# Cosine attention and a leaky-ReLU MLP on one core: another order of the norms, loads and score tiles around the first two batches

## The chip, the cores and the metric

The kernel runs on one core of a Trainium2 chip. The metric is the device time of one execution in microseconds (us). The engines are TensorE (PE), VectorE (DVE), ScalarE (ACT), GpSimd (POOL) and SyncE (SP); each takes its instructions in the order in which the kernel writes them. DMAs are issued by SP and GpSimd (and a few at the start and end by ACT) and run on the core's 16 DMA engines.

## The reference

```python
q, k, v: (8, 12, 448, 64)     # batch, heads, tokens, head_dim, float32
q_n = q / (norm(q, axis=-1) + 1e-6);  k_n = k / (norm(k, axis=-1) + 1e-6)
scores = matmul(q_n, k_n.T) / tau                       # tau = 0.1
attn = exp(scores - max) ; attn = attn / (sum + 1e-9)
a = matmul(attn, v)                                     # per head
x = a.transpose(0, 2, 1, 3).reshape(3584, 768)
h = x @ w_in                                            # 768 x 2048
out = maximum(0.01 * h, h) @ w_out                      # 2048 x 768, float32
```

## The kernel before

The unit of the attention is a *pair* of heads, numbered `s` from 0 to 47: six pairs to a batch (`NPAIR` = 6). Three *slots* `j` of two pairs each make up a batch (`NQ` = 3). A head's 448 tokens are three tiles of 128 keys and a remainder of 64; the remainders of two pairs share one tile. The order of all instructions is written out by hand, and the helpers only record them.

What is done for a pair:

- **Loads.** `load_qk(s)` issues four DMAs on SP (L142, L143, L145 twice) into one of six places of `raw_sb`. `load_pairs(eng, x, part, s, n)` loads the same for `n` pairs at once, on any engine (L127, L132).
- **Norm.** `squares(s)` on GpSimd (L182), `sums(s)` on DVE (L193), `roots(s)` on ACT in two steps (L200, L201), `normalise(s)` on DVE (L217, L218, L222 twice). For pairs from 10 on, `transposes(s)` is one DMA transpose issued by SP (L254) into `qkT[s]`. `norm(s)` records roots, normalise and transposes, then the loads of a later pair, then `hold` (a small GpSimd copy, L514, that makes GpSimd wait for the normalise), then the squares of the pair two further on.
- **Scores.** `key_tiles([(s, ki), ...])` records the score matmuls (L280) and, for each tile, an Exp on ACT (L292) to `pe`, or to `pr` for the remainder tile (`ki` = 3, of pairs `s − 1` and `s`). Each tile takes two PSUM banks from `banks(2)`, which gives out the banks that were used longest ago.
- **Products.** For a slot: `totals` (sums of the Exps by ones, L320), `reciprocals` (ACT Ln and Exp, L339 and L340), `products` with v (L320) and `scale` (DVE, L361) into `xT`. `attend_two(j)` does two slots at once, the remainder products first (`rem_products`, L307), which read `v_rem`.

The MLP works on eight chunks of tokens, alternately 384 and 512 wide, one for each batch. `firsts(b)` are the first products (L384) of chunk `b`, in 16 steps `m`, with a leaky ReLU on ACT (L391); with each step it can call other functions, by the dictionary `between`. `visit(b, ...)` are the second products (L459) of chunk `b` in groups of two 64-row halves, and between their steps the score tiles of the batch `b + 1`; `norms[i, n]` are functions called after step `n` of group `i`, and `wide`, `three`, `four`, `four_late` say after which steps a score tile stands. At a group's end its rows are copied to `osb` (DVE L471, for the last group one of two on ACT L471) and stored by SP (L436).

So the loop over the batches is: `visit(b)`, `attend_batch(b + 1)`, the loads of v (GpSimd, L160 and L167), `firsts(b + 1)`. Ahead of it stand the first batch's attention and `firsts(0)`. There, slot 2's first two MLP tiles are begun early: `begin(m, kts)` records a few of the six accumulating matmuls of tile `m`, for which the first slots' results suffice.

Before the change, pair 12 and 13 are loaded by SP in `norm(11)`, in the first visit; 14 and 15 in `attend_batch(1)`, where `norm(12)` stands too. Pairs 13 to 16 are normalised during `firsts(1)`, pair 17 in the second visit, whose last remainder tile `(17, 3)` comes at its end and whose schedule is `four_late`. From the third visit on, all remainder tiles stand at a visit's start.

Of the kernel before, what the change touches and what calls it, by code (L numbers as in the profile page):

```python
# [16 lines left out]
def kernel(  # L17
# [21 lines left out]
    NQ = NPAIR // 2  # L39
    KT = D_model // 128  # L40
# [4 lines left out]
    SOON = 4  # L45
# [20 lines left out]
    gp = nc.gpsimd  # L66
# [70 lines left out]
    def load_qk(s):  # L137
        if s >= NSLOT:
            return
        b, h0 = s // NPAIR, 2 * (s % NPAIR)  # L140
        both = raw_sb[:, s % NPAIR]
        nc.sync.dma_start(out=both[:, :, 0:3], in_=main(q, b, h0, 2))  # L142
        nc.sync.dma_start(out=both[:, :, 4:7], in_=main(k, b, h0, 2))  # L143
        for i, x in enumerate((q, k)):
            nc.sync.dma_start(  # L145
                out=both[64 * i : 64 * i + 64, :, 3],
                in_=x[b, h0 : h0 + 2, MAIN:S].rearrange("h p d -> p h d"),
            )
        raw[s] = (both[:, :, 0:4], both[:, :, 4:7])
# [36 lines left out]
    def sums(s, parts=(0, 1)):  # L186
        if s >= NSLOT:
            return
        if s not in ss:
            ss[s] = smp.tile([128, 14], F32, name="ss")  # L190
        for i in parts:
            o = ss[s][:, 0:8] if i == 0 else ss[s][:, 8:14]
            nc.vector.tensor_reduce(  # L193
                o.rearrange("p (h t) -> p h t", h=2), sqs[s][i], axis=AX.X, op=ALU.add
            )

    def roots(s):
        if s >= NSLOT:
            return
        nc.scalar.activation(ss[s], ss[s], func=AF.Ln, bias=tiny)  # L200
        nc.scalar.activation(ss[s], ss[s], func=AF.Exp, scale=0.5)  # L201
# [63 lines left out]
    def scores(s, kis):  # L265
        key_tiles([(s, ki) for ki in kis])

    def key_tiles(which):

        tiles = []  # L270
        for s, ki in which:
            sc = banks(2)
            tiles.append(sc)
            for i in range(2 if ki == 3 else 1):
                x = qkT[s - 1 + (i ^ s // 2 % NQ % 2)] if ki == 3 else qkT[s]
                for a in range(2):
                    rows = slice(64 * a, 64 * a + 64)
                    out = sc[64 * i : 64 * i + 64] if ki == 3 else sc
                    c0, c1 = (448, 512) if ki == 3 else (512 + 128 * ki, 640 + 128 * ki)
                    nc.tensor.matmul(  # L280
                        out=out[:, a, :S], lhsT=x[rows, c0:c1], rhs=x[rows, 0:S],
                        start=True, stop=True,
                    )
        for (s, ki), sc in zip(which, tiles):
            if ki == 3:
                pr[s // 2] = prp.tile([128, 2, S], BF16, name="pr")
                dst = pr[s // 2]
            else:
                if s not in pe:
                    pe[s] = pep.tile([128, 3, 2, S], BF16, name="pe")  # L290
                dst = pe[s][:, ki]
            nc.scalar.activation(out=dst, in_=sc[:, :, :S], func=AF.Exp, scale=inv_tau)  # L292
# [344 lines left out]
    def begin(m, kts):  # L637

        if (0, m) not in pms:
            pms[0, m] = banks(1, (0, m, 0))  # L640
        first(0, m, kts)

    scores(5, (0, 1))
    products(1, 1)
    for m in range(2):
        begin(m, range(2))
    for e in range(2):
        scale(1, e)
    scores(5, (2,))
    for m in range(2):  # L650
        begin(m, range(2, KT - 2))
    scores(5, (3,))
    for m in range(2, SOON):
        pms[0, m] = banks(1, (0, m, 0))
    begin(2, range(KT - 2))
    sums(6)
    sums(7)
    roots(6)

    def attend(j, behind=()):  # L660
        totals(j)
        reciprocals(j)
        po = banks(2)
        for e in range(2):
            products(j, e, po[:, e])
        for fn in behind:
            fn()
        for e in range(2):
            scale(j, e)
# [18 lines left out]

    def attend_batch(b):
        if b == 1:  # L690
            load_qk(14)
            load_qk(15)
            sums(12)
        attend_two(b * NQ)
        if b == 1:
            norm(12)
        attend(b * NQ + 2)


    def norm(s, transposed=True):  # L700
        if s >= NSLOT:
            return
        roots(s)
        normalise(s)
        if transposed:
            transposes(s)
        if s == 10:
            return
        for x in (12, 13) if s == 11 else (s + 4,) if s > 11 else ():
            load_qk(x)  # L710
        hold(qn[s][:, 6, 0, 0:1])
        if s == 11:
            squares(12)
        if s != 9:
            squares(s + (3 if s < 9 else 2))
# [11 lines left out]
    def visit(b, order, norms, between):  # L727


        s0 = (b + 1) * NPAIR  # L730
        tiles = [(s0 + p, ki) for p in range(NPAIR) for ki in range(3)]
        key_tiles([(s0 + 1, 3), (s0 + 3, 3)] + [(s0 + 5, 3)] * (b > 1))
        for i, (pairs, after) in enumerate(zip(order, between)):
            last = i == len(order) - 1
            for n, _ in enumerate(groups(b, pairs, 4 if len(pairs) > 1 else 1, last), 1):
                for _ in range(after.get(n, 0)):
                    key_tiles([tiles.pop(0)])
                for fn in norms.get((i, n), ()):
                    fn()
        assert not tiles  # L740
        if b < 2:
            key_tiles([(s0 + 5, 3)])

    def at(*steps):
        return {n: steps.count(n) for n in steps}
# [1 line left out]
    wide = (at(8, 13, 18, 24, 29, 35, 40, 45, 50, 55, 60), at(4, 8, 12, 16, 16, 21, 26))  # L747
    three = (at(9, 16, 16, 21, 26, 31), at(5, 10, 16, 16, 21, 26, 31), at(5, 10, 16, 16, 20))
    four = (at(9, 16, 16, 24), at(4, 10, 16, 16, 24), at(4, 10, 16, 16, 24), at(5, 10, 16, 16))
    four_late = (at(5, 11, 16, 16, 24),) * 3 + (at(6, 16, 16),)  # L750

    deals["apart"] = False
    attend(NQ - 1, [lambda m=m: first(0, m, range(KT - 2)) for m in range(3, SOON)])
    normalise(6)
    hold(xT[0][:, 2 * NQ - 2, 0:1])
    load_w_out(range(0, MT, MT // 4))
# [8 lines left out]
            8: [lambda: transposes(7)],  # L765
            9: [lambda: norm(9, False)],
            10: [lambda: transposes(8)],
            11: [lambda: sums(10), lambda: load_v(3)],
            12: [lambda: norm(10), lambda: load_v(4)],
            13: [lambda: transposes(9), lambda: load_v(5), lambda: load_v_rem(1)],  # L770
            15: [lambda: sums(11)],
        },
# [1 line left out]
    ready = 10  # L774
    for b in range(B):
        tokens = chunk_cols(b)[1] // 128
        if b == B - 1:
            for ts in range(tokens):
                for half in range(2):
                    second(b, ts, half)  # L780
            break
        order = [[((ts, 0), (ts, 1))] for ts in range(tokens)]
        if b == 0:
            order = [order[0] + order[1], order[2]]
        norms = {(0, 18): [lambda: norm(11)]}
        if b:
            norms = {}
            for i in range(tokens - 1 + (b == 1)):
                norms[i, 4 if tokens > 3 else 12] = [lambda s=ready: norm(s)]
                ready += 1  # L790
                norms[i, 20] = [lambda s=ready: sums(s)]
        else:
            ready += 2
        visit(
            b, order, norms,
            wide if b == 0 else four_late if b == 1 else three if tokens == 3 else four,
        )
        attend_batch(b + 1)
        for j in range((b + 2) * NQ, (b + 3) * NQ):
            load_v(j)  # L800
        load_v_rem(b + 2)
        s = ready
        between = {0: [lambda s=s: norm(s)], 1: [lambda s=s: sums(s + 1)]}
        if b == 0:
            between = {
                0: [lambda: sums(13)], 1: [lambda: norm(13), lambda: sums(14)],
                4: [lambda: norm(14), lambda: sums(15)], 7: [lambda: norm(15)],
                9: [lambda: sums(16)], 11: [lambda: norm(16)], 14: [lambda: sums(17)],
            }
            ready += 5  # L810
        elif tokens == 3:
            between.update({
                4: [lambda s=s: norm(s + 1), lambda s=s: sums(s + 2)],
                7: [lambda s=s: norm(s + 2), lambda s=s: sums(s + 3)],
                10: [lambda s=s: norm(s + 3)], 13: [lambda s=s: sums(s + 4)],
            })
            ready += 4
        else:
            between.update({
                4: [lambda s=s: norm(s + 1)], 5: [lambda s=s: sums(s + 2)],  # L820
                8: [lambda s=s: norm(s + 2)], 12: [lambda s=s: sums(s + 3)],
            })
            ready += 3
        firsts(b + 1, 0, between)
# [35 lines left out]
```

## Time and profile before

| | us |
|---|---|
| median of 3 runs (lowest to highest) | 407.20 (407.15 to 407.24) |
| profiled execution | 407.09 |
| its span | 405.3 |
| PE busy (share of the span) | 398.5 (98%) |
| ACT busy | 265.0 (65%) |
| DVE busy | 187.7 (46%) |
| GpSimd busy | 140.7 (35%) |

Where the stretches that the diff touches lie in the span: the last slot's scores of batch 0 and the early MLP products from 28 to 36 us; `firsts(0)` from 36 to 50; the first visit from 50 to 70; `attend_batch(1)` from 70 to 76.7; `firsts(1)` from 76.8 to 97.6; the second visit from 97.6 to 122.7.

How to read it: the profile is of one execution, and the time around the span (407.09 − 405.3 = 1.8 us) belongs to each run. Busy times are shares of the whole span; what an edit is worth is read in its own stretch, by what the instructions there wait for. A row of a timeline is start, duration, engine, line, operation, output and inputs with their shapes, the number of merged instructions, and in brackets idle time just before it and what ended that. `q0` is GpSimd's DMA queue, `q1` that of SP.

### The profile page before, as it was taken

How to read it: one execution, taken by the hardware profiler on the slowest of the kernel's cores; microseconds unless marked ns; L12 is line 12 of the kernel's file. 1: busy time of each engine (PE TensorE's matmuls, PEld its weight loads, DVE VectorE, ACT ScalarE, POOL GpSimd, SP SyncE). 2: the span in 40 equal slices, each digit the busy share in tenths (PEclk: the TensorE clock that was granted, in tenths of full speed). 3: DMA queues.
4: the chain of work that ended last, by engine and by line, in shares of the span. 5: the costliest groups of instructions: out<-in, count | busy, mean ns of one | idle time of the engine just before them, and what ended most of it. 6: DMA issues, size and time to landing. Idle time of an engine off the chain costs nothing.

```text
span 405.3 us, 10173 instructions
## 1 busy us (share of the span) xinstructions
PE 398.5 (98%) x4096; PEld 225.0 (56%) x4096; DVE 187.7 (46%) x403; ACT 265.0 (65%) x458; POOL 140.7 (35%) x215
## 2 busy tenths in 40 slices
PE   8999999999999999999999999999999999999996
PEld 3335655544555655544886555544687555544564
DVE  6987912684665624454452626256361731130021
ACT  5996799556874689654876569745786559844300
POOL 4995823363344513343141513255122500000000
PEclk9999999999999999999999999999999999999999
DMA  7999999697689826576486844686477721110033
GB/s 190 252 227 246 214 184 212 180 182 180 147 195 154 153 60 175 118 126 174 73 185 142 131 113 118 160 117 152 68 177 125 96 45 40 40 41 2 0 78 79
DMA packets 100735, 54.21 MB, mean 134 GB/s; under 512 B 69424, under 2 KB 95440, under 8 KB 100688
## 3 DMA queue, kind: packets, MB, share of 16 engines
q1 hardware_dynamic: 76400, 40.13, 42.0%
q0 software_dynamic: 23440, 12.92, 23.2%
q8 instruction: 32, 0.52, 0.5%
q10 hardware_dynamic: 848, 0.52, 0.4%
q14 instruction: 15, 0.12, 0.1%
HBM read 45.61 MB, written 11.01 MB: 140 GB/s over the span
## 4 chain that ended last, share of the span: by engine, by line
PE 93%; POOL 3%; DVE 1%; DMA 1%; issue 1%; ACT 0%; POOLq 0%
PE ps L384 36%; PE ps L459 31%; PE ps L320 11%; PE ps L280 8%; PE ps L421 5%; POOL sq L182 1%; PE ps L307 1%; DMA raw_sb<-in_k_dram 1%; POOL v_rem L167 1%; DVE qn L222 1%; PE ps L236 1%; POOL raw_sb L132 0%; POOL v_b L160 0%; POOL seen L514 0%; DVE qkT L261 0%
## 5 line engine op out<-in xcount | busy, mean ns | idle before, releaser
L384 PE MATMUL ps<-xT,w_in_sb 128*128 128x384 bf16 (+1 forms) x768 | 148.0, 353 | 0.0
L459 PE MATMUL ps<-w_out_sb,hT 64*128 64x384 bf16 x1536 | 144.0, 323 | 0.0
L292 ACT ACTIVATE pe<-ps 128x896 bf16<-128x896 f32 x144 | 124.5, 917 | 17.2 <-PE ps L280 15.3
L384 PEld LDWEIGHTS <-w_in_sb 128*128 128x128 bf16 x768 | 74.0, 98 | 71.7 <-issue 4.0
L391 ACT ACTIVATE hT<-ps 128x384 bf16<-128x384 f32 (+1 forms) x128 | 67.2, 544 | 66.6 <-PE ps L384 66.1
L459 PEld LDWEIGHTS <-hT 64*128 64x128 bf16 x1536 | 84.4, 94 | 44.8 <-PE ps L459 4.2
L182 POOL TENSOR_TENSOR sq<-raw_sb 128x512 f32<-128x512 f32 x90 | 82.4, 937 | 12.5 <-DMA raw_sb<-in_k_dram 11.9
L222 DVE TENSOR_TENSOR qn<-raw_sb,r 128x512 bf16<-128x512 f32 x96 | 56.6, 631 | 2.0 <-DMA raw_sb<-in_q_dram 0.3
L280 PE MATMUL ps<-qkT 64*128 64x448 bf16 (+1 forms) x384 | 54.8, 353 | 1.1 <-DVE qkT L261 0.6
L193 DVE TENSOR_REDUCE ss<-sq 128x6 f32<-128x384 f32 (+1 forms) x95 | 54.3, 610 | 1.1 <-POOL sq L182 1.0
L471 DVE COPY osb<-ps 128x384 f32<-128x384 f32 x41 | 21.2, 553 | 69.7 <-PE ps L459 38.8
L514 POOL CAST seen<-qn 128x1 f32<-128x1 bf16 x46 | 9.1, 198 | 124.3 <-DVE qn L222 124.0
L217 DVE TENSOR_SCALAR ss<-ss 128x14 f32<-128x14 f32 x48 | 10.2, 213 | 75.7 <-ACT ss L201 75.6
L361 DVE TENSOR_TENSOR xT<-ps,rb 128x448 bf16<-128x448 f32 x48 | 27.8, 620 | 24.6 <-ACT rb L340 24.4
L160 POOL DMA_DIRECT2D v_b<-in_v_dram x24 | 18.6, 776 | 39.6 <-PE ps L320 39.6
L320 PE MATMUL ps<-pe,v_b 128*32 128x448 bf16 x576 | 32.0, 353 | 0.0
L280 PEld LDWEIGHTS <-qkT 64*128 64x128 bf16 (+1 forms) x384 | 17.7, 97 | 17.6 <-issue 7.3
L339 ACT ACTIVATE rb<-ps 128x448 f32<-128x448 f32 x24 | 12.9, 538 | 14.9 <-PE ps L320 13.9
L320 PEld LDWEIGHTS <-v_b 128*32 128x32 bf16 x576 | 15.1, 97 | 12.0 <-issue 0.6
L427 DVE COPY osb<-ps 128x384 f32<-128x384 f32 (+1 forms) x9 | 4.6, 513 | 36.6 <-PE ps L421 36.6
L421 PE MATMUL ps<-w_out_sb,hT 128*128 128x384 bf16 (+1 forms) x144 | 21.0, 308 | 0.0
L292 ACT ACTIVATE pr<-ps 128x896 bf16<-128x896 f32 x24 | 20.7, 924 | 0.2 <-PE ps L280 0.2
(52 smaller groups left out, 188.2 us busy)
## 6 DMA issues: line engine op xcount, KB each, us to landing
raw_sb<-in_q_dram SPq DMA_DIRECT2D x46, 192.0 KB, 3.2
raw_sb<-in_k_dram SPq DMA_DIRECT2D x44, 192.0 KB, 3.2
out_dram<-osb SPq DMA_DIRECT2D x30, 192.0 KB, 3.0
v_b<-in_v_dram POOLq DMA_DIRECT2D x24, 192.0 KB, 4.9
out_dram<-osb SPq DMA_DIRECT2D x12, 384.0 KB, 2.6
w_out_sb<-in_moe_w_out_dram POOLq DMA_DIRECT2D x4, 768.0 KB, 15.8
w_in_sb<-in_moe_w_in_dram POOLq DMA_DIRECT2D x3, 512.0 KB, 8.4
w_in_sb<-in_moe_w_in_dram POOLq DMA_DIRECT2D x2, 768.0 KB, 12.7
```

The lines of the kernel that those rows point to most:

```text
L182: eng.tensor_tensor(sq, x, x, op=ALU.mult)
L193: nc.vector.tensor_reduce(o.rearrange("p (h t) -> p h t", h=2), sqs[s][i], axis=AX.X, op=ALU.add)
L222: scalings[s] = nc.vector.tensor_tensor(qn[s][:, lo:hi], x.rearrange("p h t d -> p t h d"), r[:, r0 : r0 + 2 * nt].rearrange("p (h t) -> p ...
L280: nc.tensor.matmul(out=out[:, a, :S], lhsT=x[rows, c0:c1], rhs=x[rows, 0:S], start=True, stop=True,)
L292: nc.scalar.activation(out=dst, in_=sc[:, :, :S], func=AF.Exp, scale=inv_tau)
L320: nc.tensor.matmul(out=x[32 * g : 32 * g + 32, :S], lhsT=weights(g, ki) if ki < 3 else rem(g), rhs=pe[s][:, ki, a, :] if ki < 3 else pr[j] ...
L361: scalings[j, e] = nc.vector.tensor_tensor(xT[m][:, 2 * jj + e, half * S : (half + 1) * S], pos.pop((j, e))[:, :S], rbs[j], op=ALU.mult,)
L384: nc.tensor.matmul(out=pm[:, :n], lhsT=w_in_sb[:, kt, m * 128 : (m + 1) * 128], rhs=xT[c // 2][:, kt, c0 : c0 + n], start=(kt == 0), stop= ...
L391: nc.scalar.activation(out=hT[c][:, m, :n], in_=pms.pop((c, m))[:, :n], func=AF.Prelu, alpha=0.01)
L421: nc.tensor.matmul(out=po2[:, :n], lhsT=hT[c][:, m, ts * 128 : (ts + 1) * 128], rhs=w_out_sb[:, m, lo : lo + n], start=(m == 0), stop=(m = ...
L459: done[p][i] = nc.tensor.matmul(out=pos2[p][:, i, :HALF], lhsT=hT[c][rows, m, ts * 128 : (ts + 1) * 128], rhs=w_out_sb[rows, m, half * HAL ...
L471: copy(out=osb[c, ts][:, half * HALF : (half + 1) * HALF], in_=po2[:, i, :HALF])
```

## The change

It has four parts. In the head, the scores of slot 2 come ahead of some of the early MLP products, and `roots(6)` is recorded after the slot's `attend`. Pairs 12 and 13 are loaded by GpSimd in `firsts(0)` at step 11, ahead of v and v_rem, with four DMAs of two pairs each; `norm(11)` then loads 14 and 15 on SP, so that `attend_batch(1)` loads nothing. The norms move up by one place: `sums(12)` and `norm(12)` into the second group of the first visit (steps 6 and 14), 13 into `attend_batch(1)`, 14 to 17 into `firsts(1)`. The second visit then takes all three remainder tiles first, normalises three pairs instead of four, and has the schedule `four` of the later visits.

```diff
     scores(5, (0, 1))
     products(1, 1)
-    for m in range(2):
-        begin(m, range(2))
+    begin(0, range(2))
     for e in range(2):
         scale(1, e)
     scores(5, (2,))
-    for m in range(2):
-        begin(m, range(2, KT - 2))
+    begin(1, range(2))
+    begin(0, range(2, KT - 2))
     scores(5, (3,))
+    begin(1, range(2, KT - 2))
     for m in range(2, SOON):
         pms[0, m] = banks(1, (0, m, 0))
-    begin(2, range(KT - 2))
+    begin(2, range(2))
     sums(6)
     sums(7)
-    roots(6)
...
         if b == 1:
-            load_qk(14)
-            load_qk(15)
-            sums(12)
+            sums(13)
         attend_two(b * NQ)
         if b == 1:
-            norm(12)
+            norm(13)
         attend(b * NQ + 2)
...
-        for x in (12, 13) if s == 11 else (s + 4,) if s > 11 else ():
+        for x in (14, 15) if s == 11 else (s + 4,) if s > 11 else ():
             load_qk(x)
...
-        key_tiles([(s0 + 1, 3), (s0 + 3, 3)] + [(s0 + 5, 3)] * (b > 1))
+        key_tiles([(s0 + 1, 3), (s0 + 3, 3)] + [(s0 + 5, 3)] * (b > 0))
...
-        if b < 2:
+        if b == 0:
             key_tiles([(s0 + 5, 3)])
...
-    four_late = (at(5, 11, 16, 16, 24),) * 3 + (at(6, 16, 16),)
...
-    attend(NQ - 1, [lambda m=m: first(0, m, range(KT - 2)) for m in range(3, SOON)])
+    attend(NQ - 1, [lambda: first(0, 2, range(2, KT - 2)), lambda: first(0, 3, range(KT - 2))])
+    roots(6)
     normalise(6)
...
-            11: [lambda: sums(10), lambda: load_v(3)],
-            12: [lambda: norm(10), lambda: load_v(4)],
+            11: [lambda: sums(10)] + [
+                lambda part=part, x=x: load_pairs(gp, x, part, 12, 2) for part in range(2) for x in (q, k)
+            ],
+            12: [lambda: norm(10), lambda: load_v(3), lambda: load_v(4)],
             13: [lambda: transposes(9), lambda: load_v(5), lambda: load_v_rem(1)],
...
-        norms = {(0, 18): [lambda: norm(11)]}
+        norms = {
+            (0, 18): [lambda: norm(11)], (1, 6): [lambda: sums(12)], (1, 14): [lambda: norm(12)],
+        }
         if b:
             norms = {}
-            for i in range(tokens - 1 + (b == 1)):
+            for i in range(tokens - 1):
...
-            ready += 2
-        visit(
-            b, order, norms,
-            wide if b == 0 else four_late if b == 1 else three if tokens == 3 else four,
-        )
+            ready += 4
+        visit(b, order, norms, wide if b == 0 else three if tokens == 3 else four)
...
-                0: [lambda: sums(13)], 1: [lambda: norm(13), lambda: sums(14)],
-                4: [lambda: norm(14), lambda: sums(15)], 7: [lambda: norm(15)],
-                9: [lambda: sums(16)], 11: [lambda: norm(16)], 14: [lambda: sums(17)],
-            }
-            ready += 5
+                0: [lambda: sums(14)], 1: [lambda: norm(14), lambda: sums(15)],
+                4: [lambda: norm(15), lambda: sums(16)], 7: [lambda: norm(16), lambda: sums(17)],
+                10: [lambda: norm(17)], 13: [lambda: sums(18)],
+            })
+            ready += 4
```

More of the change, by code (lines that the diff above doesn't have):

```diff
@@ L804 @@
         if b == 0:
-            between = {
-                0: [lambda: sums(13)], 1: [lambda: norm(13), lambda: sums(14)],
-                4: [lambda: norm(14), lambda: sums(15)], 7: [lambda: norm(15)],
-                9: [lambda: sums(16)], 11: [lambda: norm(16)], 14: [lambda: sums(17)],
-            }
-            ready += 5
+            between.update({
+                0: [lambda: sums(14)], 1: [lambda: norm(14), lambda: sums(15)],
[3 more added lines that the diff above has]
+            ready += 4
         elif tokens == 3:
```

## The prediction

> **What bounds the kernel now.** I read the page's busy times and slices first, then the chain of waits in order of time, then the timelines of TensorE (PE), ScalarE (ACT) and the DMA queues in the three stretches that the diff touches.
>
> ```profile
> span 405.3 us, 10173 instructions
> PE 398.5 (98%) x4096; PEld 225.0 (56%) x4096; DVE 187.7 (46%) x403; ACT 265.0 (65%) x458; POOL 140.7 (35%) x215
> PE   8999999999999999999999999999999999999996
> PEclk9999999999999999999999999999999999999999
> DMA  7999999697689826576486844686477721110033
> ```
>
> PE is busy 98% at the full granted clock, so only time in which PE stands can be won, and every new wait of PE is lost for good. I therefore took the matmuls' starts from the trace and looked for each that follows its predecessor later than its columns explain. After 36 us there is none over 0.13 us, and those of about 0.1 us stand wherever the shape changes (64 to 128 rows of the array and back). The sum of all excess from 12 us to the end is 9.0 us, nearly all of it such changes, which both kernels have.
>
> The last real wait is at 35.79 us. In the chain it parts these two pieces of L384, whose matmuls else start 0.163 apart:
>
> ```profile
> 34.86 0.92 PE ps L384 x5
> 35.79 2.27 PE ps L384 x13
> ```
>
> The last of the five (35.453) is followed after 0.339 instead of 0.163: it waits for the scaled products of slot 2 (DVE L361, 34.58 to 35.74).
>
> **The head: −0.18 us.** Two matmuls of `begin(0)`/`begin(1)` go from before `totals(2)` to behind `products(2)`. `totals(2)` starts 2 × 0.163 = 0.33 us sooner, and so do ACT's Ln and Exp of it (33.40 and 33.97), whose two `roots(6)` steps (0.30 + 0.21 from 32.61) now stand behind them. The scaling starts 0.33 sooner, at 34.26, and ends at 35.4, while PE still comes to the final k steps at 35.45 and 35.62: the 0.176 us wait is gone. What is moved ahead finds its bank free: the scores that start 0.33 us sooner, at 29.96 and 31.01, need the Exps that end at 29.66 and 30.47. The pr Exp then ends at 32.4, needed at 32.7. `roots(6)` at 34.13 to 34.65 is awaited by `normalise(6)` after the scaling (35.4): cover 0.7 us. Bounds: 0 to −0.18; I take −0.18.
>
> **The second batch's visit (b = 1): −0.08 us.** It gets the shape of the later four-tile visits: three remainder tiles first, none at its end, schedule `four`. Both shapes are in this trace:
>
> ```profile
> 97.60 0.57 PE L280 MATMUL ps<-qkT 64*64 64x448 bf16 x8
> 122.42 0.38 PE L280 MATMUL ps<-qkT 64*64 64x448 bf16 x4
> 122.73 0.39 PE L307 MATMUL ps<-pr,ones 64*32 64x448 bf16 x8
> ...
> 192.05 0.76 PE L280 MATMUL ps<-qkT 64*64 64x448 bf16 x12
> 217.09 0.38 PE L307 MATMUL ps<-pr,ones 64*32 64x448 bf16 x8
> ```
>
> From first remainder tile to first L307: 122.73 − 97.60 = 25.13 now, 217.09 − 192.05 = 25.04 in the new shape. The difference, 0.08 to 0.09, is the change of shape that goes. The condition is that pair 17 is transposed by 97.6. Norms 14 to 17 now stand at steps 1, 4, 7, 10 of `firsts(1)`; in the later visits of this shape they stand at 0, 4, 7, 10, and there the last transpose is issued 16.8 us after the first product (188.05 against 171.29), 4.0 us ahead of the tiles. GpSimd is fuller here (v loads until 83.8), so I work it out: squares(16) 84 to 86, sums and root(16) until 87.5, transpose(16) at 89.2, four loads behind it on SP at 0.6 each, transpose(17) at 93.0, landed 3.2 later (as 91.24 to 94.45) at 96.2: 1.4 us of cover.
>
> **The first visit (b = 0): +0.45 us.** `sums(12)` and `norm(12)` come into its second group, steps 6 and 14. DVE pays 1.14 + 0.17 + 0.24 + 1.16 us, and is idle there from 64.60 to 70.07: nothing. ACT pays two steps of L200/L201 between the Exps of (10,1) and (10,2). It has no room:
>
> ```profile
> 64.32 5.86 ACT L292 ACTIVATE pe<-ps 128x896 bf16<-128x896 f32 x7 [0.57 <-PE ps L280]
> 70.05 0.51 ACT L471 COPY osb<-ps 128x384 f32<-128x384 f32 x1
> 70.41 0.97 ACT L292 ACTIVATE pr<-ps 128x896 bf16<-128x896 f32 x1
> ...
> 70.41 0.65 PE L307 MATMUL ps<-pr,v_rem 64*32 64x448 bf16 x16
> ```
>
> Seven Exps run end to end, 0.80 to 0.86 apart, right into the copy of the finished rows, which ends at 70.557; and the second half of the sixteen v_rem matmuls starts at 70.608 and waits for ACT's semaphore: its bank is the one just copied. The same two root steps inside such a row of Exps cost 0.448 (55.310 to the next Exp at 55.758). So the copy ends at 71.0, PE starts those matmuls at 71.06, and stands 0.45 us; nothing behind it has slack to give that back. The norm's other steps: transpose(12) and load 16 go on SP ahead of the third store, which comes some 3 us later (its buffer, one of three, is next written at 103); the hold and squares(14) on GpSimd come at 69 to 72, after load 14 has landed, and their sums are due at 77.8. Bounds: 0 (if the copy's delay were covered) and 0.51 (both steps in full); I take 0.45.
>
> **Loads 12 and 13 by GpSimd: nothing, but barely covered.** Four DMAs, 2 × 384 and 2 × 64 KB, enter GpSimd's queue ahead of v 3 to 5 and v_rem; SP loses the eight that it issued from 58.98, and loads of 14 and 15 take those places. Issue costs GpSimd 4 × 0.7 us, in a stretch where it waits anyway. The queue is the matter:
>
> ```profile
> q0 software_dynamic: 1623, 1.88, 102.6%
> q1 hardware_dynamic: 806, 0.21, 20.4%
> v_b<-in_v_dram POOLq DMA_DIRECT2D x3, 192.0 KB, 12.7
> v_rem<-in_v_dram POOLq DMA_DIRECT2D x2, 32.0 KB, 12.8
> qkT<-qn SPq DMA_TRANSPOSE x2, 8.9
> ```
>
> That is the DMA part for 47.9 to 58.9: GpSimd's queue is never empty, still busy with w_out. The new 896 KB, at the 325 to 347 KB that such loads moved per us from 38 to 40, take 2.6 us of it. Three things wait behind.
> - v_rem: its last part landed at 65.1, needed at 70.41 (70.7 with ACT's delay). Plus 2.6 is 67.7. Its 768 packets, 770 per us alone, now share with 768-byte load packets of SP (464 per us alone): 290 pairs per us, 1.7 us more; v_b's sharing adds about 1. So 67.7 to 70.4, I take 69.7.
> - Transpose of pair 11: landed 64.9, first needed at 66.64. Packets of the two queues went one for one (196 and 197 in the us from 56), so the transpose of 10 is held back by about 2.3 us; the 2.2 us in which its queue was empty (59.2 to 61.4) absorb most of it. 65 to 67.5, I take 65.9.
> - squares(12): due by 63.9, so that sums(12) (1.14) are done when ACT comes to the roots at 66.84. The v_rem parts wait for the completion semaphores of w_out's last part (59.0) and of the new loads (60 to 61.7), so GpSimd comes to them at 62.4.
>
> On how the queues share, the Trainium skill ("DMA: Bandwidth & Descriptors", section on queues, rings and completion order) says that a DMA engine goes round robin between queues packet by packet; by that rule larger packets of GpSimd's queue slow a transpose more, and the trace's one-for-one counts agree. The same page (anatomy of one GpSimd DMA) fits 2.0 us + bytes / 436e3 per us, an estimate of 2.9 us for each 384 KB load; by it these loads would land before 54 and the first rival would fall away, the sum staying as it is. The trace disagrees: the two such loads issued at 29 us took 12.7 and 13.0 us to land.
>
> **Sum.** 407.09 (the profiled execution, span 405.3 and 1.8 around it) − 0.18 − 0.08 + 0.45 = 407.28. The median of the runs, 407.20, is 0.11 above it: 407.4. That is a change of 0.05%; a measurement of this kernel can tell about 0.2% (0.8 us) from none.
>
> **Rivals.**
> 1. The DMA cover fails. If v_rem lands after 70.7, or the transpose of 11 after 67.1 (the first 0.45 us of its delay lie beside ACT's), each us beyond is a us of PE. For it: saturated queue, covers of 1 us and less. Against: my middle values hold. With 1 us of error on v_rem's latest bound: 71.4 − 70.7 = +0.7; the transpose: 67.5 − 67.1 = +0.4; together up to +1.1, middle 0.5: 407.9. The half over +0.6 is the slower case: from a v_rem landing of 71.3 the kernel is over 408.0. By the page's packet rule this rival is where the change would be hurt. Chance 0.27.
> 2. GpSimd is held by its completion semaphores, squares(12) start after 63.9, ACT waits at the roots with the Exps behind it. At a start of 65.2, +1.3 us: 408.7. Against: 1.5 us of cover. Chance 0.07.
> 3. ACT's extra 0.45 is not on the path (PE's wait at 70.608 ending by DVE's copy at 70.63 shows that two copies release it): only the gains remain, 406.9. Against: ACT's copy would then have to end by 70.6. Chance 0.12.
> 4. The head's wait stays, or pair 17 is late at 97.6 by some tenths: 407.6. Chance 0.06.
>
> That the change does not do what it says can be left out: the instruction order shows the roots between the Exps of (10,1) and (10,2), three pr Exps first in the second visit, and four loads on GpSimd's queue.
>
> **How the numbers follow.** Forecast 0.48, the rivals as above. No case gains 0.8 us, as PE has no such wait to lose: faster 0.02. Over 408.0: half of rival 1 (0.13), nearly all of rival 2 (0.06): slower 0.19. Within: 0.79. The range takes in rival 3 below and most of rival 1 above: 406.9 to 408.4.
>
> **What would show it.** Right: no gap over 0.2 us in L384 near 35.5; first L307 of the second visit 25.04 after its first remainder tile; L200/L201 near 66.9 and the ACT copy ending near 70.8 (the head's gain taken off); L307 standing about half a us. Wrong: L280 waiting for qkT near 66.5, L307 for v_rem, L200 for DVE. A loss with none of these at 60 to 72 us would make my account wrong.

## The result: 0.6% slower, in four new waits of PE

| | us |
|---|---|
| before: median of 6 runs (lowest to highest) | 407.17 (406.82 to 407.24) |
| after: median of 6 runs | 409.50 (409.11 to 409.79) |
| ratio, 95% interval | 1.0059 (1.0046 to 1.0071) |
| profiled execution, before and after | 407.09, 409.33 |
| span, before and after | 405.3, 407.6 |

The forecast was 407.4, with a range to 408.4; the time lies above it. From the page of the kernel after, the lines that answer to those of before:

```profile
span 407.6 us, 10154 instructions
PE 398.7 (98%) x4086; PEld 231.5 (57%) x4096; DVE 190.1 (47%) x403; ACT 264.7 (65%) x458; POOL 144.0 (35%) x219
```

PE's busy time is the same within 0.2 us while the span has grown by 2.3: PE stands. What it stands for is in the list of PE's waits (what was waited for, us in total, times, longest); these lines are new:

```profile
PE ps L280 <- DMA qkT<-qn: 0.8, 2, 0.4
PE ps L307 <- DMA v_rem<-in_v_dram: 0.5, 1, 0.5
PE ps L459 <- DMA w_out_sb<-in_moe_w_out_dram: 0.3, 1, 0.3
```

Where they are, PE's timeline shows:

```profile
60.60 0.50 PE L459 MATMUL ps<-w_out_sb,hT 64*128 64x384 bf16 x4 [0.26 <-DMA w_out_sb<-in_moe_w_out_dram]
65.78 0.36 PE L280 MATMUL ps<-qkT 64*128 64x448 bf16 x2 [0.34 <-DMA qkT<-qn]
68.25 0.36 PE L280 MATMUL ps<-qkT 64*128 64x448 bf16 x2 [0.43 <-DMA qkT<-qn]
72.86 0.56 PE L307 MATMUL ps<-pr,v_rem 64*32 64x448 bf16 x11 [0.47 <-DMA v_rem<-in_v_dram]
```

The idle times in the brackets are counted from the modelled end of the matmul before. Counted as in the prediction, from start to start less what the columns take, the four waits are 0.43, 0.51, 0.60 and 0.63 us: 2.17 in all. (All waits below are counted in this way.) Four transfers are late, each after the other:

| | landed before | predicted | landed after | PE's wait |
|---|---|---|---|---|
| w_out's last part | 59.01 | unmoved | 60.56 | 0.43 |
| transpose of 10 | 60.29 | some 62.6 | 65.73 | 0.51 |
| transpose of 11 | 64.91 | 65.9 | 68.21 | 0.60 |
| v_rem, third and last part | 65.10 (last) | 69.7 (last) | 72.82, 73.27 | 0.63 |

With 0.21 of a wait at 46.9 us (L236 for `qn9`), which comes and goes between executions, and the gains of the head and the second visit, 2.17 + 0.21 − 0.18 − 0.08 = 2.12, against 409.33 − 407.09 = 2.24 between the two profiled executions. The loss is accounted for within 0.12 us, and the four waits lie between 60 and 73 us.

The DMA part of the kernel after, 48.9 to 59.0, the same stretch of the program as the one shown of before:

```profile
q0 software_dynamic: 1299, 2.22, 106.1%
q1 hardware_dynamic: 506, 0.13, 8.5%
v_b<-in_v_dram POOLq DMA_DIRECT2D x3, 192.0 KB, 14.7
raw_sb<-in_q_dram POOLq DMA_DIRECT2D x1, 384.0 KB, 13.4
raw_sb<-in_k_dram POOLq DMA_DIRECT2D x1, 384.0 KB, 13.8
qkT<-qn SPq DMA_TRANSPOSE x2, 12.9
```

In 10.1 us, against 11.0 before, GpSimd's queue moved more bytes (2.22 MB against 1.88), and SP's queue got 506 packets through in place of 806: the two transposes took a median of 12.9 us to land, before 8.9.

### The profile page after: what moved, and what is told of

Read it like the earlier page. It is cut to its first block, busy times and chain, and to the rows that moved or that the text cites. A ratio compares the mean times of both kernels' runs of the same rounds, so it can differ in the third digit from the quotient of the medians.

```text
span 407.6 us, 10154 instructions
## 1 busy us (share of the span) xinstructions
PE 398.7 (98%) x4086; PEld 231.5 (57%) x4096; DVE 190.1 (47%) x403; ACT 264.7 (65%) x458; POOL 144.0 (35%) x219
## 4 chain that ended last, share of the span: by engine, by line
PE 81%; DMA 11%; POOL 4%; issue 1%; SPq 1%; DVE 0%; ACT 0%; POOLq 0%
PE ps L384 32%; PE ps L459 27%; PE ps L320 10%; DMA raw_sb<-in_k_dram 9%; PE ps L280 6%; PE ps L421 5%; DMA v_rem<-in_v_dram 2%; POOL sq L182 2%; PE ps L307 1%; POOL raw_sb L132 1%; POOL raw_sb L127 1%; SPq L145 0%; POOL v_rem L167 0%; DVE qn L222 0%; POOL seen L514 0%
## 5 line engine op out<-in xcount | busy, mean ns | idle before, releaser
L384 PE MATMUL ps<-xT,w_in_sb 128*128 128x384 bf16 (+1 forms) x760 | 147.5, 352 | 0.4
L384 PEld LDWEIGHTS <-w_in_sb 128*128 128x128 bf16 x768 | 74.1, 98 | 71.6 <-issue 3.7
L459 PEld LDWEIGHTS <-hT 64*128 64x128 bf16 x1536 | 90.2, 94 | 39.3 <-PE ps L459 4.1
L222 DVE TENSOR_TENSOR qn<-raw_sb,r 128x512 bf16<-128x512 f32 x96 | 58.6, 651 | 2.0 <-DMA raw_sb<-in_q_dram 0.3
L280 PE MATMUL ps<-qkT 64*128 64x448 bf16 (+1 forms) x384 | 55.4, 352 | 2.1 <-DVE qkT L261 0.8
L217 DVE TENSOR_SCALAR ss<-ss 128x14 f32<-128x14 f32 x48 | 10.1, 210 | 78.4 <-ACT ss L201 78.3
L280 PEld LDWEIGHTS <-qkT 64*128 64x128 bf16 (+1 forms) x384 | 18.6, 97 | 17.9 <-issue 6.6
L339 ACT ACTIVATE rb<-ps 128x448 f32<-128x448 f32 x24 | 12.9, 538 | 16.5 <-PE ps L320 15.6
L167 POOL DMA_DIRECT2D v_rem<-in_v_dram x32 | 19.8, 636 | 5.7 <-DMA w_out_sb<-in_moe_w_out_dram 4.0
L427 DVE COPY osb<-ps 128x384 f32<-128x384 f32 (+1 forms) x9 | 4.6, 513 | 36.6 <-PE ps L421 36.6
```

What stands on the lines that cost most here:

```text
L222: scalings[s] = nc.vector.tensor_tensor(qn[s][:, lo:hi], x.rearrange("p h t d -> p t h d"), r[:, r0 : r0 + 2 * nt].rearrange("p (h t) -> p ...
L280: nc.tensor.matmul(out=out[:, a, :S], lhsT=x[rows, c0:c1], rhs=x[rows, 0:S], start=True, stop=True,)
L384: nc.tensor.matmul(out=pm[:, :n], lhsT=w_in_sb[:, kt, m * 128 : (m + 1) * 128], rhs=xT[c // 2][:, kt, c0 : c0 + n], start=(kt == 0), stop= ...
L459: done[p][i] = nc.tensor.matmul(out=pos2[p][:, i, :HALF], lhsT=hT[c][rows, m, ts * 128 : (ts + 1) * 128], rhs=w_out_sb[rows, m, half * HAL ...
```

## The experiments

Theory A: the four GpSimd loads slow everything else in flight, and the waits follow (the prediction's first rival, with a higher price). Rivals: the roots on ACT, GpSimd held by its semaphores, or the other parts of the change. Times are medians; beside each stands its ratio to the kernel before on the same chip, with a 95% interval.

**The loads alone (`e_gp_loads`).** The kernel before with only this:

```diff
-            11: [lambda: sums(10), lambda: load_v(3)],
-            12: [lambda: norm(10), lambda: load_v(4)],
+            11: [lambda: sums(10)] + [ ...load_pairs(gp, x, part, 12, 2) for part in range(2) for x in (q, k) ],
+            12: [lambda: norm(10), lambda: load_v(3), lambda: load_v(4)],
...
-        for x in (12, 13) if s == 11 else (s + 4,) if s > 11 else ():
+        for x in (s + 4,) if s > 11 else ():
```

> The kernel before with one part of the change: pairs 12 and 13 loaded by GpSimd at step 11 of the first products, nothing else moved (norm 12 and the loads of 14 and 15 stay where they were). Transfer theory: the 896 KB hold back w_out's last part and the transposes of 10 and 11; waits of about 0.3, 0.5 and 0.6 us at 60, 65 and 67 us, v_rem perhaps late as well: 1.0 to 2.0 us slower than before. Roots theory (the loss is ACT's two root steps in the full row of Exps): no loss, within 0.2 us of before.

408.45 us, ratio 1.0038 (1.0026 to 1.0051). Its list of PE's waits has two of the new lines:

```profile
PE ps L280 <- DMA qkT<-qn: 0.6, 2, 0.4
PE ps L459 <- DMA w_out_sb<-in_moe_w_out_dram: 0.6, 1, 0.6
```

They are 0.74 at 59.6, 0.43 at 65.0 and 0.52 at 67.3: 1.69 us. v_rem landed at 71.92, and PE did not wait for it. This one part of the change makes most of the loss.

**All but the loads (`e_no_loads`).** The kernel after without the four loads; pairs 12 and 13 take the data that lies in their places already:

```diff
-            11: [lambda: sums(10)] + [ ...load_pairs(gp, x, part, 12, 2)... ],
+            11: [lambda: sums(10), lambda: raw.update({y: raw[y % NPAIR] for y in (12, 13)})],
```

> The changed kernel without the four GpSimd loads: pairs 12 and 13 are not loaded at all, and what lies in their places (pairs 6 and 7) is used for them. Transfer theory: the four waits of 60 to 73 us go, and what is left is my sum without the rival: minus 0.18, minus 0.08, plus 0.45 for the roots, 0.2 us slower than before (2.1 us faster than the changed kernel). Roots theory: 1.5 to 2.3 us slower than before, as the changed kernel.

407.42 us, ratio 1.0011 (1.0002 to 1.0020). All four waits are gone. What is left is the prediction's ACT term, and a wait of 0.30 us for the transpose of pair 17 (told below, with the second visit). On ACT's timeline the roots stand in the row of Exps, and the copy ends at 70.82; PE's timeline has the matmuls that wait for it:

```profile
66.68 0.30 ACT L200 ACTIVATE ss<-ss,tiny 128x14 f32<-128x14 f32 x1
67.01 0.21 ACT L201 ACTIVATE ss<-ss 128x14 f32<-128x14 f32 x1
70.32 0.50 ACT L471 COPY osb<-ps 128x384 f32<-128x384 f32 x1
```

```profile
70.50 0.76 PE L307 MATMUL ps<-pr,v_rem 64*32 64x448 bf16 x16
```

L307 stands 0.24 and 0.16 us, at 70.07 and 70.53: 0.40 for 0.45 predicted.

**Without those roots too (`e_no_loads_no_roots`).**

```diff
-        roots(s)
+        if s != 12:
+            roots(s)
```

> The same without the loads of pairs 12 and 13, and also without the two root steps of pair 12 on ACT (its norm uses the sums as they are). Against the run without the loads alone it shows the price of the two root steps: 0.45 us by my sum, so 0.26 us faster than before; 0 if the copy of the rows is not on the path, then equal to that run.

407.43 us, ratio 1.0008 (0.9999 to 1.0017). The two gaps at 70 are gone from the trace, so the roots make them. The time does not show it: the medians of the two versions are the same within 0.01 us, and their intervals are about 0.4 us wide to either side. This profiled execution (407.84) had a wait of 0.61 at 46.9 for `qn9`, the one that varies between executions.

**The head alone (`e_head`).** The kernel before with the first hunks of the change, up to `roots(6)` after `attend`:

```diff
-    for m in range(2):
-        begin(m, range(2))
+    begin(0, range(2))
...
-    begin(2, range(KT - 2))
+    begin(2, range(2))
```

> The kernel before with the head's new order alone (scores of slot 2 ahead of some first products, roots(6) behind the slot). My sum: the 0.18 us wait of the first products at 35.5 us goes and nothing comes in its place, 0.18 us faster than before. Rival: the wait is made good by PE's later waits for transfers that do not move (w_out's last part at 60 us), then within 0.05 us of before.

407.02 us, ratio 1.0000 (0.9991 to 1.0009). The gap at 35.5 is gone from the trace; 0.18 us is less than the time can show.

**Half the bytes (`e_pair12`).** GpSimd loads pair 12 only; SP loads 13 and 14 in `norm(11)`, 15 and 16 in `norm(12)`:

```diff
-                lambda part=part, x=x: load_pairs(gp, x, part, 12, 2) ...
+                lambda part=part, x=x: load_pairs(gp, x, part, 12, 1) ...
-        for x in (14, 15) if s == 11 else (s + 4,) if s > 11 else ():
+        for x in (13, 14) if s == 11 else (15, 16) if s == 12 else (s + 4,) if s > 11 else ():
```

> The changed kernel with half of the GpSimd loads: pair 12 alone comes by GpSimd, 13 and 14 by SP in norm 11, 15 and 16 in norm 12. Transfer theory, delays in proportion to the bytes (with all 896 KB: w_out's last part 1.5 us, transpose of 10 about 5, transpose of 11 about 3, v_rem 7 to 8 us later than without): half of each, so w_out lands near 59.7 and the transpose of 10 near 63, both in time; transpose of 11 near 66.5, at its limit; v_rem near 69, in time. Left is the price of the roots: 0.1 to 0.5 us slower than before. If a delay comes from the loads standing in that place at all and not from their size, 1.5 to 2.3 us slower as the changed kernel.

Median 407.58, ratio 1.0029 (1.0008 to 1.0050); its executions spread from 407.10 to 411.79, and the profiled one took 409.39. In that one, slower than most, the transpose of 10 landed at 62.42, as early as in the two versions without loads (61.88 and 62.95), v_rem at 71.00, and PE waited 0.54 for the transpose of 11 (landed 67.59) and 1.04 for that of 17. Half the bytes did not delay the first transpose by half but not at all, while v_rem came 10.7 us after w_out's last part, against 7.6 and 7.8 without loads. In this one execution the delays did not go in proportion to the bytes.

**The loads behind v and v_rem (`e_loads_last`).**

```diff
-            11: [lambda: sums(10)] + [ ...load_pairs(gp, x, part, 12, 2)... ],
-            12: [lambda: norm(10), lambda: load_v(3), lambda: load_v(4)],
-            13: [lambda: transposes(9), lambda: load_v(5), lambda: load_v_rem(1)],
+            11: [lambda: sums(10), lambda: load_v(3)],
+            12: [lambda: norm(10), lambda: load_v(4)],
+            13: [lambda: transposes(9), lambda: load_v(5), lambda: load_v_rem(1)]
+                + [ ...load_pairs(gp, x, part, 12, 2)... ],
```

> The changed kernel with the four GpSimd loads behind v 3 to 5 and v_rem instead of ahead of them. Place theory: w_out's last part, the transposes and v_rem land as without the loads (59, 61 to 62, 66, 66), their waits of PE go; but GpSimd must wait for w_out and v to land before it can issue the loads, they land near 68, squares(12) end near 70, and ACT stands at the roots of pair 12 from 66.8 to about 71 with the Exps behind it: 3 to 4 us slower than before. If the mere bytes in the stretch decide and not the place, the waits at 60 to 72 us stay and the loss is 2 to 2.5 us.

416.22 us, ratio 1.0230 (1.0214 to 1.0246): 9 us slower, where 3 to 4 were expected. The transposes landed at 61.13 and 66.08 and v_rem at 68.01, with no wait for any of them. w_out's last part landed at 59.96, with no load ahead of it, and PE waited 0.30 us for it: the wait at 60 us does not need the loads. squares(12) and sums(12) came very late, and ACT stood at the roots with the Exps behind it, PE 7.25 us behind ACT:

```profile
74.38 0.31 ACT L200 ACTIVATE ss<-ss,tiny 128x14 f32<-128x14 f32 x1 [7.55 <-DVE ss L193]
```

That is the prediction's second rival, in a place where it does decide; in the kernel after it is nearly hidden (below).

**The same loads by SP (`e_loads_sp`).**

```diff
-                lambda part=part, x=x: load_pairs(gp, x, part, 12, 2) ...
+                lambda part=part, x=x: load_pairs(nc.sync, x, part, 12, 2) ...
```

> The changed kernel with the same four loads at the same step, but issued by SP, whose queue is empty there, ahead of the transpose of 10. Sharing theory (the DMA engines take turns between the queues, and w_out fills them): the loads land 5 to 6 us sooner than by GpSimd and hold w_out's last part back by some 3 us, to 62: one wait of about 2 us at 60 us, that of the transposes and of v_rem smaller: 2 to 3 us slower than before. If GpSimd's queue is what is slow, no wait at 60 us and at most 0.5 us slower than before.

411.92 us, ratio 1.0120 (1.0103 to 1.0137): 5 us slower, where 2 to 3 were expected. Nothing held SP, which issued the first load at 37.80, and they went beside w_out instead.

```profile
PE ps L459 <- DMA w_out_sb<-in_moe_w_out_dram: 3.7, 2, 1.9
```

PE waited 2.11 and 1.92 for w_out's parts. Transposes and v_rem made no wait.

**No transposes of 10 and 11 (`e_no_transposes`, `e_before_no_transposes`).** Theory A needs a reason why 896 KB cost so much. One candidate is that the transposes in flight on SP's queue slow GpSimd's. The same edit in both kernels:

```diff
         if s >= NSLOT:
             return
+        if s in (10, 11):
+            qkT[s] = qkT[s - 2]
+            return
```

> The changed kernel without the DMA transposes of pairs 10 and 11 (the transposed tiles of 8 and 9 are used in their place). It tells whether the 896 KB alone make v_rem late, or the 896 KB together with the transposes in flight: while the transpose of 10 ran, all engines together moved only 67 KB in the us from 61, against 200 and more when GpSimd's queue is alone. Bytes theory: loads land at 62 to 65, v_rem at 70 to 72, a wait for v_rem stays. Theory that a transpose in flight slows GpSimd's queue: the loads land by 61, v_rem by 68, and of the four waits only that of w_out's last part (up to 0.4 us) is left, with the 0.4 us of the roots: 0.2 to 0.7 us slower than before.

> The control: the kernel before without the same two transposes (those of 8 and 9 used in their place). Time as before within 0.2 us by both theories, since nothing waits there. Bytes theory: v_rem lands 1.5 us or less sooner than in the kernel before (65.1), by the transposes' own 448 KB. Theory that a transpose in flight slows GpSimd's queue: v 3 to 5 and v_rem land 2 us or more sooner.

410.61, ratio 1.0079 (1.0062 to 1.0096), and 409.34, ratio 1.0052 (1.0037 to 1.0067). Inconclusive in time: a DMA transpose waits for its norm, and that had held SP's later loads back. Without it SP issued them some 20 us sooner, from 41.8 and 36.6 us, and w_out came late in both kernels (waits of 3.1 and 1.5 us in all). Only differences of landings can be read: without the transposes v_rem's last part came 7.0 us after w_out's with the loads and 3.8 without them; in the kernel after it was 12.7.

**The same with SP held as before (`e_gate`, `e_before_gate`).** In place of each transpose SP issues a DMA of 512 bytes that waits for the same norm:

```diff
+        if s in (10, 11):
+            qkT[s] = qkT[s - 2]
+            nc.sync.dma_start(out=gate[:, s - 10, :], in_=qn[s][:, 6, 1, 0:2])
+            return
```

> As the changed kernel without the DMA transposes of 10 and 11, but with a small DMA (512 bytes of qn) in the place of each, so that SP comes to its next loads no sooner than it does with the transposes (without them it issued those loads 20 us sooner, and they held w_out back). Bytes theory: with the transposes gone the GpSimd queue is as late as in the changed kernel, v_rem lands 11 us or more after w_out's last part, and PE waits for it. Theory that a transpose in flight slows GpSimd's queue: v_rem lands 7 us after w_out's last part (67 to 68), and of PE's waits only up to 0.4 us for w_out and the 0.4 us of the roots are left: 0.1 to 0.7 us slower than before.

> The control: the kernel before with the same small DMAs in place of the two transposes. Time as before within 0.2 us. v_rem lands 6.1 us after w_out's last part in the kernel before; bytes theory: 5.5 to 6; theory that a transpose in flight slows GpSimd's queue: 4 us.

`e_gate` 407.39 us, ratio 1.0006 (0.9997 to 1.0016); `e_before_gate` 407.09, ratio 0.9998 (0.9988 to 1.0007). With the four loads in place and the transposes gone, all four waits are gone. Two of the four were waits for these very transposes and could not be there; what the run tells is that the loads land sooner, and that w_out's last part and v_rem are in time. v_rem came 8.8 us after w_out's last part, between the 7 of the one theory and the 11 of the other. The DMA part of `e_gate`, 48.5 to 59.0:

```profile
q0 software_dynamic: 1598, 2.54, 117.0%
v_b<-in_v_dram POOLq DMA_DIRECT2D x3, 192.0 KB, 10.8
raw_sb<-in_q_dram POOLq DMA_DIRECT2D x1, 384.0 KB, 11.3
raw_sb<-in_k_dram POOLq DMA_DIRECT2D x1, 384.0 KB, 11.5
```

Since w_out's last landing differs between executions, the landings behind it in the same queue are best counted from it:

| us after w_out's last part | loads of 12 and 13 | v_rem |
|---|---|---|
| before (transposes) | – | 6.1 |
| `e_no_loads`, `e_no_loads_no_roots` (transposes, otherwise as after) | – | 7.6, 7.8 |
| `e_before_gate` (no loads, no transposes) | – | 4.1 |
| `e_gate` (loads, no transposes) | 2.6 | 8.8 |
| `e_gp_loads` (both) | 4.8 | 11.4 |
| after (both) | 4.9 | 12.7 |

Without the transposes the loads take the 2.6 us of the prediction to the tenth (2.8 in `e_no_transposes`). Beside the transposes they take 4.8 to 4.9. The transposes' own bytes are a part of the difference: 224 KB for each, an estimate of 0.7 us at the 325 to 347 KB per us of the prediction. On v_rem the loads cost 4.7 without the transposes (8.8 − 4.1). With them, kernels that differ little but in the loads give 4.9 and 5.1 (12.7 less 7.8 and 7.6) and 5.3 (11.4 − 6.1). That is 0.2 to 0.6 more, about what single executions differ by (6.1 before, 6.6 in `e_head`), so that a further cost of the two together is not shown for v_rem.

**Another way to the second visit (`e_late_v`).** The kernel before with the head and the new visit, but no GpSimd loads: norms 13 to 17 packed into `firsts(1)`, the v loads issued late (a part of the edit):

```diff
-                0: [lambda: sums(13)], 1: [lambda: norm(13), lambda: sums(14)],
-                4: [lambda: norm(14), lambda: sums(15)], 7: [lambda: norm(15)],
-                9: [lambda: sums(16)], 11: [lambda: norm(16)], 14: [lambda: sums(17)],
+                0: [lambda: sums(13), lambda: sums(14)], 1: [lambda: norm(13)],
+                2: [lambda: norm(14), lambda: sums(15)], 5: [lambda: norm(15), lambda: sums(16)],
+                8: [lambda: norm(16), lambda: sums(17)], 11: [lambda: norm(17), loads],
+                14: [lambda: sums(18)],
```

> A version without early loads: the kernel before with the head's new order, and the second visit in its new shape (all three remainder tiles first, schedule four), reached in another way: pairs 12 and 13 stay loaded by SP in norm 11 and norm 12 stays in the attention of the second batch; all five norms 13 to 17 are packed into firsts(1), the loads of pairs 19 to 21 wait until the transpose of 17 is issued, and v 6 to 8 come behind that. By my terms minus 0.18 and minus 0.08: 0.26 us faster than before, if the transpose of 17 lands by 98.2; each us later is a us lost.

408.60 us, ratio 1.0035 (1.0022 to 1.0049): a miss. Pair 17's transpose was issued at 97.23, landed at 100.13, and PE waited 1.44 us for it.

No version ran faster than the kernel before by more than the noise; the head alone equals it.

## Why the prediction was wrong

- **The step that failed is the term "Loads 12 and 13 by GpSimd: nothing, but barely covered".** It stood in the sum at nothing; the waits that are gone without the loads are 2.17 us. It took the queue's own work rightly (2.6 us, seen in `e_gate`), added the meeting of the two queues as 2.3 us on the transpose of 10 and 2.0 on v_rem, and counted from the landings of the one profiled execution. Measured: the transpose of 10 came 5.4 us later than before, not 2.3, that of 11 3.3, not 1.0, and v_rem 8.2, not 4.6. Three things were left out or taken wrongly.
- **The landings it counted from were early ones.** In five other versions with these transposes and without the loads in that place (`e_head`, `e_no_loads`, `e_no_loads_no_roots`, `e_loads_last`, `e_late_v`; one execution each) nearly all landings are later:

| landed at, us | before | the five others | predicted | after |
|---|---|---|---|---|
| w_out's last part | 59.01 | 58.90 to 60.29 | 59.0 | 60.56 |
| transpose of 10 | 60.29 | 60.77 to 62.95 | 62.6 | 65.73 |
| transpose of 11 | 64.91 | 65.36 to 67.10 | 65.9 | 68.21 |
| v_rem, last part | 65.10 | 65.97 to 68.09 | 69.7 | 73.27 |

  They spread by 1.4 to 3.0 us, and the covers that the prediction gave v_rem and the transpose of 11 were about 1 us. Counted from w_out's last part, and against the two versions of the kernel after without the loads, the loads cost v_rem 4.9 and 5.1 us, near the predicted 4.6, and the transpose of 10 2.2 and 2.5, near the predicted 2.3 (against the kernel before it would be 3.9).
- **What transposes in flight do to GpSimd's queue was left out.** The sharing was reckoned in one direction, what larger packets do to a transpose. The loads show the other: they took 4.8 to 4.9 us where 2.6 to 2.8 are enough without transposes. How much of the lateness of each transfer is this, and how much the spread between executions, is open.
- **w_out's last part was taken as unmoved**, since it is ahead of the loads in its queue. It landed at 60.56. How much of that is the loads' is open: with no load ahead of it it landed at 60.25 and 60.29 in two executions in which w_in's last part had come late too (41.6 and 42.1, for 40.4), but at 59.96 in `e_loads_last`, where w_in's had not (40.28). Of those with the loads, the kernel after had w_in's at 41.56, and `e_gp_loads` at 40.43, with w_out's at 60.48. So 0.43 of the 2.17 us is not shown to be the loads'.
- **Rival 1 (the DMA cover fails) is what happened**, with its signs: L280 waits for qkT, L307 for v_rem. Its price was capped at 1.1 us, from an error of 1 us on v_rem's latest bound; the miss was 2.9 us (73.3 against 70.4). The waits sum to less than the delays, since the transposes and v_rem had cover, and since each wait moves PE back and so covers part of the next: v_rem's third part landed 1.8 us over the 71.06 at which PE was to come to it, and cost 0.63, since PE came to it at 72.0.
- **GpSimd (rival 2) was late, beside the other waits.** It came to squares(12) at 65.62, not 62.4, since its v_rem issues waited for the loads' late completions:

```profile
60.84 0.60 POOL L167 DMA_DIRECT2D v_rem<-in_v_dram  x1 [3.95 <-DMA w_out_sb<-in_moe_w_out_dram]
65.62 3.60 POOL L182 TENSOR_TENSOR sq<-raw_sb 128x512 f32<-128x512 f32 x4 [0.38 <-DMA raw_sb<-in_k_dram]
```

  That is 1.7 us past the due time of 63.9. But PE's first three waits had put ACT's Exps back as well: ACT came to the roots at 67.97, as sums(12) ended (68.03). So it added next to nothing here; that it would have cost about a us had the transfers been in time is an inference, and no run shows it. In `e_loads_last` the same mechanism decides.
- **The roots on ACT, +0.45**: right, 0.40 in `e_no_loads` and again in `e_gate`:

```profile
70.19 0.38 PE L311 MATMUL ps<-pr,ones 64*32 64x448 bf16 x8
70.65 0.75 PE L311 MATMUL ps<-pr,v_rem 64*32 64x448 bf16 x16
```

  (Its lines are numbered four higher.) In the kernel after it is hidden: ACT's copy ends at 72.21, v_rem lands at 72.82 and 73.27.
- **The head, −0.18**: right in the trace. The scaling starts at 34.24, predicted 34.26, and the gap in L384 is gone:

```profile
34.24 1.16 DVE L361 TENSOR_TENSOR xT<-ps,rb 128x448 bf16<-128x448 f32 x2 [1.88 <-ACT rb L340]
```

- **The second visit, −0.08**: right. From first remainder tile to first L307, 125.01 − 99.96 = 25.05, predicted 25.04:

```profile
99.96 0.76 PE L280 MATMUL ps<-qkT 64*64 64x448 bf16 x12
125.01 0.38 PE L307 MATMUL ps<-pr,ones 64*32 64x448 bf16 x8
```

  But that it cost nothing more was luck. Pair 17's transpose was to be issued at 93.0 and to land at 96.2, 1.4 us ahead of its tile. It was issued at 97.23 and landed at 100.21, just as PE, some 2 us late, came to the tile at about 100.3. Where PE was not late, the transpose was: in `e_no_loads` it was issued at 95.44 and landed at 98.45, and the same twelve matmuls took 1.06 us in place of 0.76:

```profile
97.80 1.06 PE L280 MATMUL ps<-qkT 64*64 64x448 bf16 x12
```

  That is 0.30 us, and 0.37 in `e_no_loads_no_roots`; in `e_gate` it landed 0.2 us ahead. This is the second half of rival 4, and it is more than the visit gains.

Without these transposes the rest of the sum held: `e_gate`'s ratio of 1.0006 (0.9997 to 1.0016) contains the forecast 1.0005. That tests the head, the visits and the roots together, not the term that failed, which had the widest bounds and whose middle values were the ones that cost nothing.

## What to carry to other kernels

Where a transfer joins a full DMA queue while another engine's queue has DMA transposes in flight, do not price the delay by bytes and a rate alone: here 896 KB took 4.9 us in place of 2.6, and a transpose in the other queue came 5.4 us later. Reckon the cover of each transfer that is waited for in that stretch, those ahead in the queue among them, and take the landings from several executions (here they spread by up to 3 us), and give several covers of about 1 us a common chance of failing, not one each. A cover that holds only since the engine is late elsewhere, as that of pair 17 here, is none. And before a transfer is moved to another engine's queue, or taken out, ask what held its issue back: SP without a waiting instruction sent loads some 20 us too soon, into the weights' way.

## What the runs showed of the hardware

- **While both queues had work throughout, their packets went one for one, whatever their size.** Each us from 55 to 60 of the kernel after, q0 and q1 moved 108 and 108, 103 and 104, 108 and 107, 134 and 135, 149 and 151 packets. Before the change it was 196 and 197 in the us from 56, with packets of 384 to 1536 bytes on q0; the loads' are 4608. So a transpose's 256-byte packets went at about half the pace. The Trainium skill ("DMA: Bandwidth & Descriptors", section on queues, rings and completion order) says that an engine goes round robin between its queues, a packet at a time; these counts agree, if what the profile counts as a packet is what that page means by one.
- **That rule does not give the whole delay: with DMA transposes in flight both queues stalled for about a us, with the loads or without.** In the us from 61 the kernel after moved 70 KB in both queues together, in 75 and 79 packets, most of them of 256 and 384 bytes; `e_gate` moved 247 KB. The DMA part for this one us, with the engines' busy share in 40 slices in tenths:

```profile
DMA  9999999949953149933319210212077101010299
q0 software_dynamic: 75, 0.05, 84.2%
q1 hardware_dynamic: 79, 0.02, 80.3%
```

  A packet's time is counted in the slice in which it begins. So the low digits do not say that the engines had nothing to do: few packets began, while some 14 of each queue were in flight, for up to 0.88 us each. `e_no_loads` has a deeper stall, without any such load, while its transpose of 10 was in flight. From 60 to 61 it moved 13 KB:

```profile
DMA packets 41, 0.01 MB, mean 13 GB/s; under 512 B 41, under 2 KB 41, under 8 KB 41
```

  By the traces' records of packets, the longest one that began between 50 and 70 us took 0.76 to 1.57 us in all ten versions with the transposes of 10 and 11 (0.98 before the change, 1.07 after), and 0.14 to 0.47 in the four without. So the stall goes with the transposes and does not need the loads; before the change PE waited for none of the transfers behind it. What makes it, and how much of the 2.3 us on the loads it is, stays open. The first and the last of the sixteen completion signals of the first load came at 56.94 and 62.41: the engines were up to 5.5 us apart, in `e_gate` 3.2 (56.72 to 59.87), for a v part of before 1.3. That a transpose lets the engines that are ahead wait for those behind would fit, but no run tells it apart.
- **In a full queue the time for a load depended on what was ahead of it, hardly on its size.** The 384 KB loads took 13.4 and 13.8 us to land, and the 64 KB ones beside them 13.4 and 14.3; without the transposes it was 11.3 and 11.5, and 11.0 and 10.6. By the fit of the Trainium skill ("DMA: Bandwidth & Descriptors", section on the anatomy of one GpSimd DMA, 2.0 us + bytes / 436e3 per us) the estimate for 384 KB is 2.9; the traces disagree, as the queue here was never empty.
